# Linear attention ahead of two feed-forward layers: kv by head on 64-column tiles, mean squares on 32-column tiles, k and v loaded by head

## The chip, the cores and the metric

One core of a Trainium2 chip runs the whole program in one launch. The metric is the device time of one execution in microseconds; the time of before is the median of three runs.

## What is computed

For each of 8 batches and 8 heads (576 positions, 64 columns a head) the attention is linear: no softmax, a 64x64 matrix kv of each head, and a root-mean-square norm of each output row. Two feed-forward layers without bias follow.

```python
def _attn_ref(q, k, v, g_norm) -> np.ndarray:
    kv = np.einsum('bhsd,bhse->bhde', k, v)
    out = np.einsum('bhsd,bhde->bhse', q, kv)
    rms = np.sqrt(np.mean(out * out, axis=-1, keepdims=True) + 1e-06)
    return (out / rms * g_norm).astype(np.float32)
...
    x = np.ascontiguousarray(attn_out.transpose(0, 2, 1, 3)).reshape(B * S, H * D)
    x = _moe_ref(x=x, **moe_kwargs)      # (max(0.01*h, h) @ w_out), h = x @ w_in
    return _moe2_ref(x=x, **moe2_kwargs) # ((h - tanh(h)) @ w_out), h = x @ w_in
```

There are 4608 tokens, a model width of 512 and a hidden width of 2048; the four weight matrices come as 64-bit floats and are converted on the chip.

## The kernel before, in words

**The large products.** Each up- and down-projection is cut into blocks of two by two that are multiplied with seven products instead of eight (`PROD`, `NOP = 7`), and every f32 operand is split into two f16 parts, so that one product is a row of f16 matmuls on the whole 128x128 array (`three`, L483 to L493). `up` (L576) runs over superblocks of tokens and 8 pieces of the hidden width, 64 steps of seven products in the first layer; `down` (L641) likewise. Their results leave the banks by ScalarE (`keep`, L518) and VectorE (`add`, L531).

**The attention.** A pair of heads is worked at once (`pair`, L760). Its steps are, on TensorE: `kv` (L765), six f32 matmuls that contract 96 positions each, with both heads' k as the 128 stationary columns and both heads' v as the 128 moving ones, of whose 128x128 result only the two diagonal 64x64 blocks are used; `qtr` (L785), the transposes of q in two halves of 288 positions; `o` (L802), the output of one half with the block-diagonal kv; and `m` (L821), the mean of squares of one half, a matmul with a selecting matrix `sel` that adds the squares of one head into one row of the bank `pm`. A batch has four pairs, and `pm` collects 16 rows (8 heads by two halves) over them. After the last pair `norms` (L843) takes the root on ScalarE, three reciprocals on VectorE, stores the result to DRAM (`store`, L858), reads it back broadcast over 64 partitions in eight loads (`load`, L862), multiplies on GpSimd and splits the result into the f16 operands of the first up-projection.

**What sets the order.** All instructions are recorded in an order that a planner (`Plan`, L44) makes from assumed durations; each engine, and SyncE's DMA queue, works its list in that order and waits by semaphores. The first batch and the second stand ahead of the first product (`early_pair`, L946). The 24 pairs of batches 2 to 7 are woven into the first up-projection: `extra` (L968) puts the seven steps of a pair behind the products n0 + `OFFS` (L969), and `between1` (L987) adds their assumed durations `D_KV`, `D_Q`, `D_O`, `D_M` (L745) to the planner's time of TensorE. Loads of weight words, their conversion and their splitting are spread over that same planned time (`spread`, L1007 to L1013), some of them up to its end.

**The loads.** `load_pair` (L747) puts k, v and q of a pair into tiles of 96 partitions with 6 positions each, the two heads side by side within a position, by one DMA a head:

```python
            held[nm] = L.take([CP, NC, 2, D], F32, nm)
            for h in range(2):
                nc.sync.dma_start(
                    out=held[nm].ap[:, :, h], in_=src[b, 2 * c + h].rearrange("(p c) d -> p c d", p=CP)
                )
```

The matmul of `m` has 16 output rows; the program as built places it on a tile of 128 rows by 32 columns of the array already before the change, all other matmuls of `pair` on the whole array.

Of the kernel before, what the change touches and what calls it, by code (L numbers as in the profile page):

```python
# [11 lines left out]
F32 = mybir.dt.float32  # L12
# [17 lines left out]
P = 128  # L30
# [100 lines left out]
def body(ctx, tc, q, k, v, g_norm, w1, w2, w3, w4, out):  # L131
# [10 lines left out]
    NS2 = NT // (2 * T2)  # L142
    NU = 4 * P
    NL, NM, NX = 20, 11, 13

# [23 lines left out]

    ivd = [scratch([2 * H, T1], F32, f"iv_{b}") for b in range(B)]  # L170
    x1d = {(c, s): scratch([P, 2 * T1], F32, f"x1_{c}_{s}") for c in range(DM // P) for s in range(NS1)}
# [20 lines left out]
    mw = const.tile([P, 4, 2 * NP], F32, name="mw")  # L192
    sel = const.tile([P, 4 * H - 2], F32, name="sel")
    kvd = [const.tile([P, P], F32, name=f"kvd{n}") for n in range(2)]

    def constants():
        for h in range(2):
            nc.sync.dma_start(out=gcol[D * h:D * h + D, :], in_=g_norm.rearrange("(p o) -> p o", o=1))
        make_identity(nc, ident)
        nc.vector.memset(ones, 1.0)  # L200
        nc.vector.memset(eps_sb, EPS / (X_SCALE * X_SCALE))
        nc.vector.memset(sel, 0.0)
        for n in range(2):
            nc.vector.memset(sel[D * n:D * n + D, 2 * H - 2 + n:2 * H - 1 + n], 1.0 / D)
            nc.vector.memset(kvd[n], 0.0)
        nc.vector.tensor_reduce(out=gabs, in_=gcol, axis=AX.X, op=ALU.max, apply_absolute_value=True)
# [537 lines left out]
    PAIRS = (0, 2, 1, 3)  # L744
    D_KV, D_Q, D_O, D_M = 1.6, 0.7, 0.6, 0.55  # L745

    def load_pair(b, c, held):  # L747
        for nm, src in (("k", k), ("v", v), ("q", q)):
            held[nm] = L.take([CP, NC, 2, D], F32, nm)
            for h in range(2):  # L750
                nc.sync.dma_start(
                    out=held[nm].ap[:, :, h], in_=src[b, 2 * c + h].rearrange("(p c) d -> p c d", p=CP)
                )
# [6 lines left out]
    def pair(b, c, held):  # L760
# [4 lines left out]
        def kv():  # L765
            held["pk"], held["bank"] = att_bank("pk")
            for a in range(NC):
                nc.tensor.matmul(
                    out=held["pk"][:, :P], lhsT=two_heads(held["k"], a), rhs=two_heads(held["v"], a),
                    start=(a == 0), stop=(a == NC - 1),  # L770
                )

        def kv_after(e):
            def go():
                held["kvd"] = kvd[kv_n[0] % 2]
                kv_n[0] += 1
                for h in range(2):
                    r = slice(D * h, D * h + D)
                    nc.scalar.activation(out=held["kvd"][r, r], in_=held["pk"][r, r], func=AF.Copy)
                used.discard(held["bank"])  # L780
                L.give(held["k"])
                L.give(held["v"])
            plan.do("A", e + 0.15, 0.5, go)
# [36 lines left out]

        def m(r):  # L821
            first, last = (c == PAIRS[0] and r == 0), (c == PAIRS[-1] and r == 1)
            if first:
                pm[b] = bank(5, "pm")
            row = H * r + 2 * c
            nc.tensor.matmul(
                out=pm[b][:2 * H, :T1], lhsT=sel[:, 2 * H - 2 - row:4 * H - 2 - row], rhs=sq[r].ap,
                start=first, stop=last,
            )
            X.give(sq[r])  # L830

        def m_after(r, e):
            if c == PAIRS[-1] and r == 1:
                norms(b, e)
# [3 lines left out]
            (D_Q, lambda: qtr(1), lambda e: q_after(1, e)), (D_O, lambda: o(0), lambda e: o_after(0, e)),  # L838
            (D_O, lambda: o(1), lambda e: o_after(1, e)), (D_M, lambda: m(0), lambda e: m_after(0, e)),
            (D_M, lambda: m(1), lambda e: m_after(1, e)),  # L840
        ]

    def norms(b, e):  # L843
        held = {}

        def root():
            held["iv"] = X.take([2 * H, T1], F32, "iv")
            nc.scalar.activation(
                out=held["iv"].ap, in_=pm[b][:2 * H, :T1], func=AF.Sqrt,
                bias=eps_sb[:2 * H], scale=1.0 / (X_SCALE * X_SCALE),  # L850
            )
            used.discard(5)
# [9 lines left out]
        def load(kk):  # L862
            held[kk] = L.take([P, 4, T1], F32, "bc")
            rows = ivd[b].rearrange("(r h) t -> h r t", r=2)
            for n in range(2):
                for h in range(2):
                    nc.sync.dma_start(
                        out=held[kk].ap[D * h:D * h + D, 2 * n:2 * n + 2],
                        in_=rows[2 * (kk + 2 * n) + h:2 * (kk + 2 * n) + h + 1].broadcast_to((D, 2, T1)),
                    )  # L870
# [75 lines left out]
    def early_pair(b, c, t, held):  # L946
        gaps = (0.0, 1.7, 2.5, 3.4, 4.4, 5.2, 6.2)
        for (dur, fn, after), g_ in zip(pair(b, c, held), gaps):
            at(t + g_, fn)
            after(t + g_ + dur)  # L950
# [17 lines left out]
    extra = {}  # L968
    OFFS = (1, 4, 6, 8, 10, 12, 14)  # L969
    loads = []  # L970
# [270 lines left out]
```

## Time and profile before

| | |
|---|---|
| median of three runs | 1646.12 us (1645.23 to 1646.91) |
| the profiled execution's own time | 1649.15 us |
| its span, first to last instruction | 1647.4 us |
| TensorE matmuls busy | 1512.3 us, 92% |
| VectorE, ScalarE, GpSimd busy | 1301.6, 867.2, 746.0 us |
| granted TensorE clock, mean | 0.959 |
| DMA packets, of them under 512 B | 251578, 129440 |
| DMA, share of 16 engines | 62.7% |

Busy matmul time counts each matmul from its start to its modelled end, and matmuls overlap, so what the array takes for a group of them is better read from the starts of neighbouring groups. A wait in the profile is the idle time of an engine ahead of an instruction, with what ended it. A queue of SyncE ("SPq") only issues transfers; the time from issue to landing is not in its rows.

### The profile page before, as it was taken

The numbers are of one execution on the slowest core, as the hardware profiler recorded it, in microseconds if no ns is written. First come the engines' busy times: TensorE is split into PE (matmuls) and PEld (weight loads), VectorE is DVE, ScalarE is ACT, GpSimd is POOL, SyncE is SP. The second block draws the span as 40 slices with busy tenths as digits, with TensorE's granted clock in tenths as the row PEclk, the third lists the DMA queues.
The fourth block names the chain that finished last, engine by engine and source line by source line (L and its number), as shares of the span: only waits on it lengthen the run. The fifth ranks groups of instructions, "written<-read, shape, count | busy, mean of one in ns | idle before, by whom it ended". The sixth has DMA issues, their size and how long they took to land. (4 is left out here: it accounts for less than half of the span.)

```text
span 1647.4 us, 32120 instructions
## 1 busy us (share of the span) xinstructions
PE 1512.3 (92%) x12274; PEld 1227.4 (75%) x12274; DVE 1301.6 (79%) x2113; ACT 867.2 (53%) x1381; POOL 746.0 (45%) x758
## 2 busy tenths in 40 slices
PE   5299898898989999999999979999999889999998
PEld 3156675666767777777777768888888778888887
DVE  4765676576667778889989669999999988888881
ACT  3366454465655664444444246666776645455441
POOL 0356203144143345666656134446887654444440
PEclk8589999999999999999999989999999999999999
DMA  9856897898896885545455565555666844444441
GB/s 210 172 88 160 227 239 208 245 245 235 252 259 209 282 318 168 185 145 200 155 172 173 184 233 206 186 210 196 243 240 243 316 143 143 157 129 135 145 132 33
DMA packets 251578, 322.08 MB, mean 196 GB/s; under 512 B 129440, under 2 KB 194080, under 8 KB 251424
## 3 DMA queue, kind: packets, MB, share of 16 engines
q1 hardware_dynamic: 251424, 320.03, 62.7%
q8 instruction: 96, 1.57, 0.4%
q14 instruction: 58, 0.48, 0.1%
HBM read 190.84 MB, written 129.12 MB: 194 GB/s over the span
## 5 line engine op out<-in xcount | busy, mean ns | idle before, releaser
L489 PEld LDWEIGHTS <-w 128*128 128x128 f16 x8400 | 824.8, 99 | 280.1 <-issue 98.7
L468 POOL TENSOR_TENSOR gl<-gl 128x256 f32<-128x256 f32 (+1 forms) x272 | 309.5, 1138 | 307.2 <-issue 79.9
L489 PE MATMUL ps_c<-ops,w 128*128 128x288 f16 (+1 forms) x2400 | 337.3, 285 | 40.2 <-DVE g L536 28.2
L489 PE MATMUL ps_a<-ops,w 128*128 128x288 f16 (+1 forms) x2400 | 333.6, 284 | 22.2 <-ACT u L527 10.3
L489 PEld LDWEIGHTS <-ops 128*128 128x128 f16 x1728 | 169.8, 98 | 28.8 <-issue 7.7
L372 POOL TENSOR_TENSOR unit<-unit 128x128 f32<-128x128 f32 x192 | 134.1, 699 | 116.0 <-DVE wo L365 97.4
L489 PE MATMUL ps_b<-opa,w 128*128 128x288 f16 (+1 forms) x1200 | 170.2, 287 | 0.0
L489 PE MATMUL ps_a<-opa,w 128*128 128x288 f16 (+1 forms) x1200 | 166.8, 283 | 2.9 <-DMA w<-wd 2.8
L489 PE MATMUL ps_d<-opa,w 128*128 128x288 f16 (+1 forms) x1200 | 165.9, 282 | 2.7 <-DVE g L536 2.7
L468 DVE TENSOR_TENSOR gl<-gl 128x256 f32<-128x256 f32 (+1 forms) x272 | 156.0, 576 | 3.3
L874 POOL TENSOR_TENSOR xg<-xg,bc 128x1152 f32<-128x1152 f32 x16 | 43.1, 2694 | 254.3 <-DMA bc<-iv 208.7
L1145 POOL TENSOR_TENSOR g<-g,th 128x512 f32<-128x512 f32 x72 | 101.0, 1403 | 95.9 <-ACT th L1142 95.7
L431 ACT ACTIVATE ops<-gl,inv 128x1024 f16<-128x1024 f32 x72 | 82.6, 1147 | 110.2 <-POOL gl L468 102.9
L489 PEld LDWEIGHTS <-opa 128*128 128x128 f16 x1296 | 126.8, 98 | 16.6 <-issue 1.9
L429 ACT ACTIVATE ops<-gl 128x1152 f16<-128x1152 f32 x64 | 74.3, 1162 | 99.5 <-POOL gl L468 94.6
L438 DVE SCALAR_TENSOR_TENSOR ops<-gl,inv,ops 128x1024 f16<-128x1024 f32 x72 | 104.4, 1451 | 15.8 <-ACT ops L431 15.4
L436 DVE TENSOR_TENSOR ops<-gl,ops 128x1152 f16<-128x1152 f32 x64 | 99.8, 1559 | 19.9 <-ACT ops L429 19.7
L365 DVE SCALAR_TENSOR_TENSOR wo<-unit,s_w,wo 128x384 f16<-128x384 f32 (+1 forms) x96 | 83.4, 871 | 27.1 <-ACT wo L362 26.7
L489 PE MATMUL ps_c<-w,ops 128*128 128x256 f16 x864 | 98.4, 275 | 3.8 <-DVE osb L536 3.8
L489 PE MATMUL ps_a<-w,ops 128*128 128x256 f16 x864 | 96.1, 273 | 3.2 <-ACT u L527 3.2
L468 POOL TENSOR_TENSOR x1g<-x1g 128x256 f32<-128x256 f32 x72 | 68.1, 946 | 65.1 <-DMA x1g<-x 34.7
L438 DVE SCALAR_TENSOR_TENSOR opa<-gl,inv,opa 128x768 f16<-128x768 f32 x72 | 87.2, 1211 | 12.5 <-ACT opa L431 12.5
(118 smaller groups left out, 2192.3 us busy)
## 6 DMA issues: line engine op xcount, KB each, us to landing
g<-g SPq DMA_DIRECT2D x64, 576.0 KB, 4.4
gl<-g SPq DMA_DIRECT2D x64, 576.0 KB, 4.7
g<-g SPq DMA_DIRECT2D x72, 512.0 KB, 3.0
gl<-g SPq DMA_DIRECT2D x72, 512.0 KB, 4.5
wd<-wo SPq DMA_DIRECT2D x48, 448.0 KB, 2.8
w<-wd SPq DMA_DIRECT2D x24, 896.0 KB, 7.4
words<-in_moe_w_in_dram SPq DMA_DIRECT2D x64, 256.0 KB, 5.0
words<-in_moe_w_out_dram SPq DMA_DIRECT2D x64, 256.0 KB, 4.0
```

What stands on the lines that cost most here:

```text
L365: nc.vector.scalar_tensor_tensor(out=dst()[:, 1, a:b], in0=cols(0, n), scalar=scale(), in1=dst()[:, 0, a:b], op0=ALU.mult, op1=ALU.subtract,)
L372: nc.gpsimd.tensor_tensor(out=o, in0=a, in1=b, op=ALU.subtract)
L429: nc.scalar.activation(out=o, in_=i_, func=AF.Copy)
L431: nc.scalar.activation(out=o, in_=i_, func=AF.Identity, scale=scale())
L436: nc.vector.tensor_tensor(out=o, in0=i_, in1=h, op=ALU.subtract)
L438: nc.vector.scalar_tensor_tensor(out=o, in0=i_, scalar=scale(), in1=h, op0=ALU.mult, op1=ALU.subtract)
L468: lambda: e.tensor_tensor(out=g()[:, o], in0=g()[:, a], in1=g()[:, b], op=op),
L489: nc.tensor.matmul(out=out_, lhsT=a, rhs=c, start=start and m == 0, stop=stop and m == n - 1, skip_group_check=not fresh,)
L874: nc.gpsimd.tensor_tensor(out=x, in0=x, in1=held[kk].ap, op=ALU.mult)
L1145: e.tensor_tensor(out=g()[:, n], in0=g()[:, n], in1=held["t"].ap[:, n], op=ALU.subtract)
```

## The change

- `load_pair`: k and v lie in their tiles head by head (96 x 2 x 6 x 64), so that a partition's six positions of one head are one run of 1536 B on both sides of the DMA; q stays as it was.
- `kv`: one matmul of each head with 64 stationary and 64 moving columns in place of one with 128 by 128 for both; head 0 on the array's columns 0 to 63, head 1 on 64 to 127, into partitions 0 to 63 and 64 to 127 of the bank, alternating; 12 f32 matmuls instead of 6.
- `m`: both halves in one step, on array columns 0 to 31 and 32 to 63; `pm`, the inverse norms and their DRAM tile get 64 rows (32 a half, of which 8 are used) instead of 16.
- The planner's durations and slots: kv 0.9 instead of 1.6, a transpose 0.5 instead of 0.7, the one m 0.7 instead of two of 0.55; six steps a pair behind products 1, 4, 6, 8, 10 and 13 instead of seven behind 1, 4, 6, 8, 10, 12 and 14.

```diff
+    Q = 32
...
-    ivd = [scratch([2 * H, T1], F32, f"iv_{b}") for b in range(B)]
+    ivd = [scratch([2 * Q, T1], F32, f"iv_{b}") for b in range(B)]
...
-    sel = const.tile([P, 4 * H - 2], F32, name="sel")
+    sel = const.tile([P, 2 * Q - 2], F32, name="sel")
...
-    D_KV, D_Q, D_O, D_M = 1.6, 0.7, 0.6, 0.55
+    D_KV, D_Q, D_O, D_M = 0.9, 0.5, 0.6, 0.7
...
-            held[nm] = L.take([CP, NC, 2, D], F32, nm)
+            apart = nm != "q"
+            held[nm] = L.take([CP, 2, NC, D] if apart else [CP, NC, 2, D], F32, nm)
...
-                    out=held[nm].ap[:, :, h], in_=src[b, 2 * c + h].rearrange("(p c) d -> p c d", p=CP)
+                    out=held[nm].ap[:, h] if apart else held[nm].ap[:, :, h], in_=src[b, 2 * c + h].rearrange("(p c) d -> p c d", p=CP)
...
             for a in range(NC):
-                nc.tensor.matmul(
-                    out=held["pk"][:, :P], lhsT=two_heads(held["k"], a), rhs=two_heads(held["v"], a),
-                    start=(a == 0), stop=(a == NC - 1),
-                )
+                for h in range(2):
+                    nc.tensor.matmul(
+                        out=held["pk"][D * h:D * h + D, :D], lhsT=held["k"].ap[:, h, a], rhs=held["v"].ap[:, h, a],
+                        start=(a == 0), stop=(a == NC - 1), tile_position=(0, D * h), skip_group_check=True,
+                    )
...
-                    nc.scalar.activation(out=held["kvd"][r, r], in_=held["pk"][r, r], func=AF.Copy)
+                    nc.scalar.activation(out=held["kvd"][r, r], in_=held["pk"][r, :D], func=AF.Copy)
...
-        def m(r):
-            first, last = (c == PAIRS[0] and r == 0), (c == PAIRS[-1] and r == 1)
+        def m():
+            first, last = c == PAIRS[0], c == PAIRS[-1]
...
-            row = H * r + 2 * c
-            nc.tensor.matmul(
-                out=pm[b][:2 * H, :T1], lhsT=sel[:, 2 * H - 2 - row:4 * H - 2 - row], rhs=sq[r].ap,
-                start=first, stop=last,
-            )
-            X.give(sq[r])
+            for r in range(2):
+                nc.tensor.matmul(
+                    out=pm[b][Q * r:Q * r + Q, :T1], lhsT=sel[:, Q - 2 - 2 * c:2 * Q - 2 - 2 * c], rhs=sq[r].ap,
+                    start=first, stop=last, tile_position=(0, Q * r), skip_group_check=True,
+                )
+                X.give(sq[r])
...
-            (D_O, lambda: o(1), lambda e: o_after(1, e)), (D_M, lambda: m(0), lambda e: m_after(0, e)),
-            (D_M, lambda: m(1), lambda e: m_after(1, e)),
+            (D_O, lambda: o(1), lambda e: o_after(1, e)), (D_M, m, m_after),
...
-        gaps = (0.0, 1.7, 2.5, 3.4, 4.4, 5.2, 6.2)
+        gaps = (0.0, 1.2, 2.0, 2.9, 3.9, 5.7)
...
-    OFFS = (1, 4, 6, 8, 10, 12, 14)
+    OFFS = (1, 4, 6, 8, 10, 13)
```

How the instructions move, first on TensorE, at the first products of the up-projection (ps_a and ps_b are the products' banks, pk the bank of kv, pm that of the mean squares; the last pair of the second batch ends here and the first woven one begins). Before:

```order
L489 MATMUL ps_b<-opa,w_0_688 128x288
L768 MATMUL pk<-v,k 128x128 x6
L826 MATMUL pm<-sq,sel 16x288
L489 LDWEIGHTS w_0_688
L489 MATMUL ps_a<-ops,w_0_688 128x288
```

and with the change:

```order
L490 MATMUL ps_b<-opa,w_0_712 128x288
L829 MATMUL pm<-sq,sel 32x288 x2
L771 MATMUL pk<-v,k 64x64 x12
L490 LDWEIGHTS w_0_712
L490 MATMUL ps_a<-ops,w_0_712 128x288
```

Before, the first half's pm stood one product earlier and the second half's stood alone behind kv; now both halves stand together, here ahead of kv.

Second, on SyncE's DMA queue, around the store of the second batch's inverse norms (iv), the broadcast loads that read it (bc), the loads of a pair (k, v, q), of weight words, and the stores of results (g1) and converted weights (wf). Before:

```order
L302 DMA words_1772<-in_moe_w_out_dram 128x2x256 x2
L751 DMA k_1800<-in_k_dram 96x6x64 x2
L751 DMA v_1803<-in_v_dram 96x6x64 x2
L751 DMA q_1806<-in_q_dram 96x6x64 x2
L859 DMA iv_2_71<-iv_1741 16x288
L867 DMA bc_1837<-iv_2_71 64x2x288 x4
L606 DMA g1_0_7_116<-g_1643 128x1152
L347 DMA wf_1_0_1_246<-unit_1763 128x512
L867 DMA bc_1877<-iv_2_71 64x2x288 x4
L302 DMA words_1883<-in_moe_w_out_dram 128x2x256 x2
```

and with the change:

```order
L303 DMA words_1821<-in_moe_w_out_dram 128x2x256 x2
L753 DMA k_1867<-in_k_dram 96x384 x2
L753 DMA v_1870<-in_v_dram 96x384 x2
L753 DMA q_1873<-in_q_dram 96x6x64 x2
L861 DMA iv_2_71<-iv_1796 64x288
L869 DMA bc_1910<-iv_2_71 64x2x288 x4
L303 DMA words_1941<-in_moe_w_out_dram 128x2x256 x2
L869 DMA bc_1948<-iv_2_71 64x2x288 x4
L348 DMA wf_1_0_0_245<-unit_1834 128x512
L607 DMA g1_0_7_116<-g_1710 128x1152
```

The next words now stand between the two groups of broadcast loads instead of behind them, and the stores of results and weights come later. From the end of the first up-projection on, every engine's list is the same as before.

## Rows read from the trace of the kernel before

**Rows 1.** Busy time by stretches; behind the clock: share of 16 DMA engines, GB/s

```profile
core 0: us, PE busy (x) PEld busy (x) DVE busy (x) ACT busy (x) POOL busy (x), PEclk, DMA share, GB/s
0.00:47.00 47.00, 29.31 (x103) 19.93 (x104) 23.23 (x61) 15.53 (x36) 0.70 (x6) 0.78 0.93 219
47.00:58.00 11.00, 0.54 (x2) 0.00 (x0) 11.00 (x29) 5.30 (x8) 0.00 (x0) 0.61 0.49 151
...
80.00:100.00 20.00, 15.28 (x59) 8.84 (x59) 11.74 (x15) 11.76 (x26) 16.59 (x25) 0.65 0.85 115
105.00:590.00 485.00, 449.97 (x3324) 332.79 (x3324) 326.62 (x635) 275.33 (x529) 157.59 (x183) 0.96 0.80 231
```

**Rows 2.** TensorE's waits, 105 to 590 us: total us, times, longest

```profile
PE ps_c L489 <- DVE g L536: 18.5, 8, 5.9
PE ps_a L489 <- ACT u L525: 9.1, 3, 3.8
```

**Rows 3.** ScalarE's waits that a late load or GpSimd ended, same stretch

```profile
ACT wo L362 <- DMA unit<-wf: 22.4, 3, 8.8
ACT opa L429 <- POOL xg L874: 14.3, 10, 3.5
ACT unit L314 <- DMA words<-in_moe_w_out_dram: 13.6, 3, 8.2
```

**Rows 4.** SyncE's DMA queue in order of time: start, us of issuing, count

```profile
169.41 0.33 SPq L606 DMA_DIRECT2D g<-g  x1
...
172.80 1.27 SPq L751 DMA_DIRECT2D k<-in_k_dram  x2
...
177.12 0.83 SPq L859 DMA_DIRECT2D iv<-iv  x1
181.06 2.57 SPq L867 DMA_DIRECT2D bc<-iv  x4
```

**Rows 5.** All engines in order of time, 186 to 197 us; in brackets: idle before

```profile
188.57 1.23 SPq L302 DMA_DIRECT2D words<-in_moe_w_out_dram  x2
...
194.56 0.67 ACT L314 ACTIVATE unit<-words 128x512 f32<-128x512 f32 x1 [8.20 <-DMA words<-in_moe_w_out_dram]
```

**Rows 6.** TensorE in order of time, 300.5 to 318 us: start, us to the modelled end

```profile
300.58 0.91 PE L489 MATMUL ps_a<-ops,w 128*128 128x288 f16 x6
301.42 0.66 PE L826 MATMUL pm<-sq,sel 128*16 128x288 f32 x2
302.01 0.91 PE L489 MATMUL ps_c<-ops,w 128*128 128x288 f16 x6
302.75 0.90 PE L489 MATMUL ps_b<-opa,w 128*128 128x288 f16 x6
...
304.92 1.50 PE L768 MATMUL pk<-v,k 96*128 96x128 f32 x12
306.26 0.90 PE L489 MATMUL ps_d<-opa,w 128*128 128x288 f16 x6
...
311.91 0.65 PE L804 MATMUL po<-qt,kvd 128*128 128x288 f32 x2
312.39 0.90 PE L489 MATMUL ps_d<-opa,w 128*128 128x288 f16 x6
```

**Rows 7.** TensorE's waits, 0 to 67 us

```profile
PE pk L768 <- DMA v<-in_v_dram: 10.8, 2, 7.9
```

**Rows 8.** In order of time: ScalarE's first split of weights, TensorE's first product

```profile
67.38 0.61 ACT L362 ACTIVATE w<-w1f,s1g 128x384 f16<-128x384 f32 x1 [12.58 <-DVE s1g L268]
...
105.32 0.90 PE L489 MATMUL ps_a<-opa,w 128*128 128x288 f16 x6
```

**Rows 9.** Loads of weights: group of products, and by tile (ns min/median/max)

```profile
L489 PEld LDWEIGHTS <-w 128*128 128x128 f16 x8400 | 824.8, 99 | 280.1 <-issue 98.7
...
L768 PEld LDWEIGHTS pk<-v,k x384: 186/192/338, 7.9 to 491.9; 96*128 96x128 f32 x192
...
L826 PEld LDWEIGHTS pm<-sq,sel x128: 92/95/151, 14.0 to 504.0; 128*16 128x16 f32 x128
```

More of the change, by code (lines that the diff above doesn't have):

```diff
@@ L203, in constants @@
         for n in range(2):
-            nc.vector.memset(sel[D * n:D * n + D, 2 * H - 2 + n:2 * H - 1 + n], 1.0 / D)
+            nc.vector.memset(sel[D * n:D * n + D, Q - 2 + n:Q - 1 + n], 1.0 / D)
             nc.vector.memset(kvd[n], 0.0)
@@ L819, in o_after, with m_after @@
             plan.do("V", end, 0.46, copy)
-        def m(r):
-            first, last = (c == PAIRS[0] and r == 0), (c == PAIRS[-1] and r == 1)
+        def m():
+            first, last = c == PAIRS[0], c == PAIRS[-1]
             if first:
                 pm[b] = bank(5, "pm")
-            row = H * r + 2 * c
-            nc.tensor.matmul(
-                out=pm[b][:2 * H, :T1], lhsT=sel[:, 2 * H - 2 - row:4 * H - 2 - row], rhs=sq[r].ap,
-                start=first, stop=last,
-            )
-            X.give(sq[r])
-        def m_after(r, e):
-            if c == PAIRS[-1] and r == 1:
+            for r in range(2):
[4 more added lines that the diff above has]
+                X.give(sq[r])
+        def m_after(e):
+            if c == PAIRS[-1]:
                 norms(b, e)
@@ L846, in root @@
         def root():
-            held["iv"] = X.take([2 * H, T1], F32, "iv")
+            held["iv"] = X.take([2 * Q, T1], F32, "iv")
             nc.scalar.activation(
-                out=held["iv"].ap, in_=pm[b][:2 * H, :T1], func=AF.Sqrt,
-                bias=eps_sb[:2 * H], scale=1.0 / (X_SCALE * X_SCALE),
+                out=held["iv"].ap, in_=pm[b][:2 * Q, :T1], func=AF.Sqrt,
+                bias=eps_sb[:2 * Q], scale=1.0 / (X_SCALE * X_SCALE),
             )
@@ L863, in load @@
             held[kk] = L.take([P, 4, T1], F32, "bc")
-            rows = ivd[b].rearrange("(r h) t -> h r t", r=2)
+            rows = ivd[b].rearrange("(r q) t -> q r t", r=2)
             for n in range(2):
```

## The prediction

> **What bounds the kernel now.** I read the busy time by stretches first [rows 1]. The program has two parts for this change: everything up to 105 us, in which the first batch's attention and the first weights are prepared, and the first up-projection from 105 to 590 us, in which the attention of batches 2 to 7 is woven between the products. Behind 590 us the order of every engine's instructions is the same as before, so what is gained or lost ahead of it is carried to the end. In the 485 us of the up-projection TensorE is busy 450 us: it is the bound. What it idles there shows in its waits [rows 2]: the two largest groups hold 27.6 us, and they name VectorE and ScalarE. Those two are not slow, they are held up: ScalarE idles for loads that come late [rows 3], 22.4 us for halves of weights, 13.6 us for weight words and 14.3 us for the scaled attention output, which itself waits for a load. ScalarE and VectorE work their lists in order, so a late load at the head of the list holds back the evictions behind it, and TensorE waits for a bank. One such place is told in full by the list of the DMA queue [rows 4] and the engines beside it [rows 5]: around 172 to 191 us the queue issues loads of the next pair, the store of the inverse norms, the broadcast loads and then weight words; the words issued at 188.57 us are what ScalarE had been idle for 8.20 us for, up to 194.56 us. So two things cost time here: TensorE's own stream, and the crowded DMA queue.
>
> **TensorE, kv.** The stream is read from a quiet stretch [rows 6]. Six products with 288 columns take 0.74 us (302.01 to 302.75). The twelve matmuls of one kv (six f32 matmuls, two instructions each) take 306.26 - 304.92 = 1.34 us, 0.112 each, with no gap ahead or behind. After the change there are 24 instructions with half the columns, so 0.056 us each. If the two heads' tiles work at once, each head's chain is 12 x 0.056 = 0.67 us, and the second starts one instruction later: 0.73 us. If they don't, it is 24 x 0.056 = 1.34 us. To this comes a change of tile shape on the way in and out. The kernel has one already: the matmul of the mean squares writes 16 rows and is built on a 128x32 tile, and it takes 302.01 - 300.58 - 0.74 = 0.69 us, while two f32 matmuls of the same 288 columns on the whole array (o, 311.91 to 312.39) take 0.48. The difference, 0.21 us, is 0.10 ahead (the six products from 300.58 end their stream at 301.32, pm starts at 301.42) and 0.11 behind. I take it for kv too: 0.73 + 0.21 = 0.94 us, a gain of 0.40; without overlap 1.55, a loss of 0.21.
>
> **TensorE, mean squares.** Now 2 x 0.69 = 1.38 us a pair. After the change both halves stand in one place, so one of the two switches goes. Without overlap: 4 x 0.24 + 0.21 = 1.17 us, a gain of 0.21. With overlap I count that the two instructions of one half stay in order on their tile and the other half's first starts with the second of these: 3 x 0.24 + 0.21 = 0.93, a gain of 0.45. No row shows whether two column tiles work at once, that is the main unknown; between 0.85 gained and nothing (0.21 - 0.21) a pair, I take the overlap, because the row nearest to it, pm on its narrow tile, runs its two instructions back to back at the full column rate once the tile shape is set. 24 pairs stand in the up-projection: **24 x 0.85 = 20.4 us less**, bounds 0 and 24 x 1.35 = 32 (both halves in 0.48 us and kv in 0.67, no switch at kv). Loads of weights cost nothing in these counts, since today a product's load of 99 ns [rows 9] is hidden at a pitch of 0.123 us [rows 6]. The Trainium skill (TensorE: Matmul & The Clock Gate, Part 3: Packing small matmuls, on what overlaps) speaks against that: a load overlaps matmuls in flight only where the row groups differ, and here all are the same. The products of this trace disagree for the whole array; for column tiles no row decides. By the rows the term stays at 20.4 us less, by the rule it would be the slow rival's 89 us more. The other eight pairs run ahead of 105 us, where TensorE waits for loads and ScalarE anyway; I cost them at nothing.
>
> **The loads of k and v.** A load of one head of k moves 96 x 6 x 64 x 4 B = 147 KB. Now its pieces are 256 B, after the change each partition's 1536 B are one run on both sides. Between 80 and 100 us hardly anything but such loads is on the queue: 115 GB/s at a share of 0.85, or 135 GB/s at a full share; between 47 and 58 us the pieces are 1 KB: 151 GB/s at 0.49, or 308 [rows 1]. Shares are rough at the edges of a stretch, but a factor of two is safe. Four such loads a pair, 24 pairs, are 14.2 MB: 105 us of full DMA time become 46, out of 0.80 x 485 = 388. The queue's issues get shorter too: a load whose pieces are strided takes 1.27 us for two, a store with one run a partition 0.33 for one [rows 4].
>
> What that is worth in the up-projection is an estimate. The 27.6 us of waits follow from late loads, but part of their chain stays: store of the norms, then broadcast loads, then GpSimd. I take a quarter off, with a little more for TensorE's clock, which was granted at 0.96 on the mean [rows 1], and give back what a faster TensorE adds by arriving earlier: **6 us less**; bounds 17 less (all late words gone) and 10 more. For the "more" speaks that the planner now counts 3.8 us a pair where it counted 5.3 (36 us over the stage), so the second weights' splitting and the third's conversion, spread up to the planned end, fall on fewer products: VectorE's 327 us [rows 1] then lie in some 458 us, 71% instead of 67%. Also m is now at slot 13 instead of 12 and 14, so the norms of a batch start one product sooner, and the words that came behind the broadcast loads now stand between them. The store of the inverse norms has 64 rows instead of 16 (74 KB, half of one k load); it lies on the chain to the broadcast loads, and I count 0.3 us of the 6 against it each time.
>
> Ahead of 105 us the DMA share is 0.93 up to 47 us [rows 1], and TensorE waits 10.8 us for v [rows 7]; behind it VectorE has the converted words to finish, the scale is ready at 67.38 us and the splits of the first weights follow [rows 8]. The 16 loads of k and v of the first batch are 2.36 MB, 17.5 us at 135 GB/s and 7.7 at 308: at most 9.8 us. VectorE's own work (23.2 us in the first 47, then all of 47 to 58) hides about half: **4.5 us less**, bounds 0 and 9.8.
>
> The sum: 20.4 + 6 + 4.5 = 30.9 us less than the profiled execution's 1649.15 us, or 1618.2; the median of the runs, 1646.12, is 3.03 below it, so **1615 us**. Square, copies and evictions keep their sizes; kvd is copied from other columns of the bank, at the same 64x64.
>
> **The rivals.**
> *The tiles don't overlap*, so the change of shape is paid and nothing bought: TensorE 0, the loads' 10.5 us stay: 1635.6 us. Against it speaks only that the pieces are on different columns of the array. A chance of 0.17.
> *Only the mean squares overlap.* For kv each instruction needs its own weights, and a load for 64 f32 columns has the same 0.056 us of columns as its matmul; if loads go one after another, kv stays at 1.55. Then 24 x (0.45 - 0.21) = 5.8 us from TensorE, 16.3 in all: 1630 us. For it: today's kv is as close to its loads as to its matmuls (192 ns a load against 95 for 16 columns [rows 9], so some 0.1 of each is columns). 0.17.
> *Slower: loads no longer hide.* Today's loads are hidden, as said. If on column tiles a load waits until the matmul ahead has left the array, each of kv's 24 instructions costs 0.056 plus a load between 0.095 and 0.192 us, say 0.14: 24 x 0.196 + 0.21 = 4.9 us, and m 4 x (0.24 + 0.095) + 0.21 = 1.55. That is 3.7 us more a pair, 89 us over 24: some 1725 us. It makes the kernel slower from 0.016 us of uncovered load an instruction on (10.5 us over 24 x 28). Against it: pm's second instruction on its narrow tile starts without such a wait, or its 0.69 us would be 0.78. The rule of the Trainium skill quoted above (TensorE: Matmul & The Clock Gate, Part 3) is this case. 0.07.
> *The waits grow instead*, by 10 us, as VectorE's list gets denser and the loads come in a new order: 1631. 0.06. *The waits mostly go*, 17 us: 1604. 0.06.
>
> **How the numbers follow.** The forecast has 0.47: overlap in both places and some relief, 1603 to 1626 by its own bounds. The range 1600 to 1638 adds the rivals up to 1636 and leaves out the slow one and the far ends of the bounds. Differences under 0.2%, about 3 us, can't be told from no change. Faster 0.89, within it 0.03 (a mixture of growing waits and no overlap), slower 0.08 (loads that don't hide, or waits much worse).
>
> **What would show it.** In the changed profile: from the start of a pk group to the next product 0.94 us and for pm 0.93, with the second tile's matmuls starting while the first's run; 1.55 and 1.17 say no overlap, near 5 says uncovered loads. 128 loads x 480 = 61,440 packets fewer; the DMA share of the up-projection near 0.72; the two largest groups of waits near 20 us instead of 27.6; the first product near 101 us instead of 105.32 [rows 8]; the part from the end of the up-projection to the end unchanged within 3 us. If TensorE's pair costs are right and the time is not, the waits or the part behind 590 us must have grown, and I would be wrong on the relief.

## The result, and the profile after

The changed kernel takes **1606.53 us** (median of four runs, 1600.36 to 1607.68) against 1646.51 us for the kernel before in the same set (1645.23 to 1648.07): a ratio of 0.9749, 95% interval 0.9722 to 0.9776. A second set, the same two kernels again below, gave 0.9744 (0.9717 to 0.9772). The forecast of 1615 us was 8.5 us too high, and the time lies inside the range. The profiled execution of the changed kernel is the fastest of the four (1600.36 us, span 1598.6).

By stretches, cut at the first product and at the end of the first up-projection (columns as in [rows 1]):

```profile
0.00:99.00 99.00, 50.60 (x304) 28.53 (x305) 68.65 (x141) 43.23 (x90) 34.06 (x52) 0.71 0.68 179
99.00:546.00 447.00, 418.82 (x3610) 313.45 (x3608) 318.27 (x631) 271.93 (x525) 158.97 (x177) 0.98 0.78 251
546.00:1598.00 1052.00, 1007.10 (x8749) 858.92 (x8746) 908.78 (x1342) 551.60 (x770) 556.76 (x530) 0.99 0.54 183
```

The up-projection takes 447 us instead of 485, 38 us less, where the medians differ by 40. Subtracting TensorE's busy time splits it: busy 449.97 [rows 1] to 418.82, 31 us less; idle 35.0 to 28.2, 7 us less. The stretches ahead and behind are 6 and 4 us shorter here, but those two differences don't hold, as a second profile of the kernel before will show.

TensorE's stream in the quiet stretch (start, us to the modelled end; beside [rows 6]):

```profile
304.14 0.90 PE L490 MATMUL ps_a<-ops,w 128*128 128x288 f16 x6
304.97 0.92 PE L771 MATMUL pk<-v,k 96*64 96x64 f32 x24
305.82 0.91 PE L490 MATMUL ps_d<-opa,w 128*128 128x288 f16 x6
...
315.39 0.90 PE L490 MATMUL ps_c<-ops,w 128*128 128x288 f16 x6
316.21 0.68 PE L829 MATMUL pm<-sq,sel 128*32 128x288 f32 x4
316.83 0.91 PE L490 MATMUL ps_b<-opa,w 128*128 128x288 f16 x6
```

Six products take 0.74 us, so kv takes 305.82 - 304.14 - 0.74 = 0.94 us, switches of tile shape included (1.34 before), and both halves of the mean squares 316.83 - 315.39 - 0.74 = 0.70 (2 x 0.69 before). In the single records of these groups kv's matmuls start in pairs, the two heads' 6 to 8 ns apart and the pairs every 58 ns (the second pair 106 ns behind the first); in pm the first instructions of both halves start 6 ns apart, and the second ones 7. Both column tiles work at once in both places.

TensorE's waits in the up-projection (total us, times, longest; beside [rows 2]), and ScalarE's (beside [rows 3]):

```profile
PE ps_a L490 <- ACT c L526: 9.3, 5, 7.0
PE ps_c L490 <- DVE g L537: 8.9, 6, 3.0
PE ps_a L490 <- ACT u L526: 3.5, 2, 1.9
PE pm L829 <- ACT sq L813: 3.5, 3, 1.3
```

```profile
ACT opa L430 <- POOL xg L876: 16.0, 7, 3.7
ACT wo L363 <- DMA unit<-wf: 11.0, 4, 5.4
...
ACT unit L315 <- DMA words<-in_moe_w_out_dram: 6.0, 8, 2.0
```

The two groups that held 27.6 us hold 12.4, and another has come up, 9.3 us for c, of which one wait is 7.0. The 3.5 us for the squares are new: m now stands one product sooner than the second half's did, and in the place at 302.79 us it is the second half's square that it waited 1.28 us for. ScalarE waits half as long for halves of weights (wo) and for the words of the down-projection, and no less for the scaled attention output (opa, which needs GpSimd's xg, the output times the inverse norms). One wait is new, 8.7 us, for words of the up-projection; with it, ScalarE's waits for weights are 35 us, against 44 before.

DMA packets (all, and under 512 B):

```profile
DMA packets 190525, 322.57 MB, mean 202 GB/s; under 512 B 55712, under 2 KB 133024, under 8 KB 190368
```

61,053 packets fewer than before, where 61,440 were counted; the other 387 are nearly the 8 x 48 rows by which the stores of the inverse norms have grown, which the count left out. Ahead of the first product (ScalarE's first split of weights; TensorE's first product; beside [rows 8]):

```profile
61.31 0.61 ACT L363 ACTIVATE w<-w1f,s1g 128x384 f16<-128x384 f32 x1 [12.09 <-DVE s1g L269]
```

```profile
98.92 0.90 PE L490 MATMUL ps_a<-opa,w 128*128 128x288 f16 x6
```

Up to 60 us TensorE's waits for v hold 10.5 us, as before [rows 7]; over all of the stretch ahead of that product they are 16.0 us, against 17.8 before.

### The profile page after: what moved, and what is told of

It reads as the page before. It is cut to its first block, busy times and chain, and to the rows that moved or that the text cites. A ratio compares the mean times of both kernels' runs of the same rounds, so it can differ in the third digit from the quotient of the medians.

```text
span 1598.6 us, 32852 instructions
## 1 busy us (share of the span) xinstructions
PE 1476.5 (92%) x12658; PEld 1200.9 (75%) x12658; DVE 1295.7 (81%) x2113; ACT 866.8 (54%) x1381; POOL 749.8 (47%) x758
## 5 line engine op out<-in xcount | busy, mean ns | idle before, releaser
L490 PE MATMUL ps_a<-ops,w 128*128 128x288 f16 (+1 forms) x2400 | 331.1, 283 | 23.3 <-ACT u L528 10.5
```

Source lines behind the costliest of these rows:

```text
L490: nc.tensor.matmul(out=out_, lhsT=a, rhs=c, start=start and m == 0, stop=stop and m == n - 1, skip_group_check=not fresh,)
```

## The experiments

Twelve runs were made: ten other kernels, and the two of this document once more. The kernel before, on the chips of these sets, had medians of 1648.72 (the first four experiments), 1648.24 (the next four) and 1647.93 us (the last four); ratios are to those.

### The parts, one at a time

**Loads alone**: the kernel before with k and v loaded head by head. kv reads 128 adjacent columns of the tiles, two positions of one head, so it leaves out the sums that the attention needs and keeps the matmuls' shapes.

```diff
-            held[nm] = L.take([CP, NC, 2, D], F32, nm)
+            apart = nm != "q"
+            held[nm] = L.take([CP, 2, NC, D] if apart else [CP, NC, 2, D], F32, nm)
...
-                    out=held["pk"][:, :P], lhsT=two_heads(held["k"], a), rhs=two_heads(held["v"], a),
+                    out=held["pk"][:, :P], lhsT=flat(held["k"], a), rhs=flat(held["v"], a),
```

> The kernel before with k and v loaded head by head and nothing else; kv's matmuls keep their shapes and read 128 columns that lie side by side in the new tiles (two positions of one head in place of one position of two heads, so kv holds other sums). Theory A, the gains add up: TensorE's stream is unchanged (kv 1.34 us, pm 0.69 us), the first product comes some 5 us earlier and the waits of the up-projection shrink by about 6 to 10 us: 1630 to 1638 us. Theory B, the loads are the main part and TensorE's time is only swapped against waits: 25 us or more off, 1622 us or less. Theory C, the loads were hidden anyway and the rest came from the planner's new numbers: within 4 us of 1646.

**Old loads**: the changed kernel with the loads of before. It has the tiles, and the planner's new durations and slots with them.

```diff
-                        out=held["pk"][D * h:D * h + D, :D], lhsT=held["k"].ap[:, h, a], rhs=held["v"].ap[:, h, a],
+                        out=held["pk"][D * h:D * h + D, :D], lhsT=held["k"].ap[:, a, h], rhs=held["v"].ap[:, a, h],
```

> The changed kernel with the loads of k and v as before (256 B pieces), the matmuls on column tiles and the planner's new numbers kept. Theory A: kv 0.95 us and m 0.71 us a pair stay, that is 25 us off TensorE's stream; the first product near 105 us and the waits as before: 1617 to 1625 us. Theory B: with the DMA queue as crowded as before, waits eat most of the 25 us: 1632 to 1640 us. Theory C as for A, but with fewer waits than before: 1612 us or less.

**Planner's durations alone**: the kernel before, its instructions and slots unchanged.

```diff
-    D_KV, D_Q, D_O, D_M = 1.6, 0.7, 0.6, 0.55
+    D_KV, D_Q, D_O, D_M = 0.9, 0.5, 0.6, 0.35
```

> The kernel before with the planner's durations of the change (kv 0.9, a transpose 0.5, the two mean squares 0.7 together) and nothing else; slots behind the products stay. Theory A and B: the order moves a little, time within 5 us of 1646. Theory C: the new order of loads and conversions is what shortens the waits: 8 us off or more, 1638 us or less.

**Heads in turn**: the changed kernel, head 0's six matmuls and then head 1's.

```diff
-            for a in range(NC):
-                for h in range(2):
+            for h in range(2):
+                for a in range(NC):
```

> The changed kernel with kv's twelve matmuls in another order: first the six of head 0, then the six of head 1, instead of alternating. If two column tiles work at once only where their matmuls stand next to each other in the list, kv goes from 0.95 to about 1.55 us, 24 x 0.6 = 14 us on TensorE, and the time to about 1618 to 1622 us. If TensorE reorders over a longer stretch or each tile has a list of its own, kv stays near 0.95 us and the time within 4 us of 1606.

Measured: loads alone 1638.92 us, ratio 0.9929 (0.9904 to 0.9954); old loads 1614.68, 0.9789 (0.9760 to 0.9818); durations alone 1640.41, 0.9950 (0.9931 to 0.9970); heads in turn 1613.89, 0.9778 (0.9749 to 0.9806). The loads by themselves gain 10 to 12 us (by medians and by the ratio), the durations by themselves 8. The tiles were run by themselves nowhere: the kernel with old loads owes its 34 us to tiles, durations and slots together, and what the durations are worth in it only the kernels further below tell. The up-projection of the loads alone, of the old loads, and of the durations alone (by stretches, as above):

```profile
99.80:584.00 484.20, 447.48 (x3324) 331.03 (x3323) 327.50 (x635) 274.63 (x529) 156.25 (x183) 0.96 0.74 231
```

```profile
101.90:557.60 455.70, 419.73 (x3611) 313.34 (x3610) 317.77 (x631) 271.99 (x525) 158.52 (x178) 0.98 0.83 247
```

```profile
103.70:583.40 479.70, 445.95 (x3323) 329.33 (x3322) 317.74 (x631) 271.65 (x525) 157.32 (x177) 0.98 0.77 232
```

With the loads alone the DMA share of the stage falls from 0.80 to 0.74, yet the stage stays at 484 us and TensorE's idle time at 484.2 - 447.5 = 36.7: the lighter queue buys no wait there. With the old loads TensorE is as little busy as in the change (419.7), and its idle time is 36.0 instead of 28.2. So the loads do take 8 us of waits away once TensorE is faster and the durations are new, and none in the old setting, by one profile of each. The ratios say the same less sharply: 0.9789 and the change's 0.9749 and 0.9744 have intervals that overlap. With the durations alone the idle time is 479.7 - 445.95 = 33.7 us, hardly less than before; what the stage is shorter there is mostly busy time, at a granted clock of 0.98.

kv with the heads in turn (TensorE in order of time):

```profile
301.57 1.43 PE L771 MATMUL pk<-v,k 96*64 96x64 f32 x24
302.94 0.91 PE L490 MATMUL ps_d<-opa,w 128*128 128x288 f16 x6
```

302.94 - 301.57 is 1.37 us, with the switch ahead 1.46 (the median of the 24 in the stage), against 0.94. So the tiles share the time only where their instructions stand close together; with the order in turn, kv is no faster than on the whole array. In the single records a head's instructions start every 58 ns, and only around the change of heads three pairs start 3 to 6 ns apart, so that the first instructions of head 1 run beside the last of head 0. That is 24 x 0.52 = 12 us, and the stage is 462.6 instead of 447. The median is 7 to 9 us above the changed kernel's, fewer than the 12; the ratio's interval overlaps that of the change at its edge. The same records tell of the weight loads: even one after another on one tile, a matmul and its load take 0.058 us, about the time of the matmul's columns alone (0.056).

### The same two kernels again

> The kernel before once more, for a second profile of it: how far the stretches differ between two profiles of one kernel. If the 5 us that the part behind the up-projection is shorter in the changed kernel's profile are the change's work, this part takes 1057 us again; if it is the spread of single executions, it takes 1050 to 1055 us.

> The changed kernel once more beside the two variants below, on their chip: a ratio of 0.972 to 0.978 to the kernel before; first product near 99 us, up-projection 447 us within 3.

Measured: before, in its profiled execution, 1644.54 us; after 1604.66, ratio 0.9744 (0.9717 to 0.9772). Before and after, by stretches:

```profile
0.00:99.60 99.60, 51.59 (x208) 33.16 (x209) 65.86 (x137) 40.17 (x85) 31.13 (x47) 0.73 0.85 177
99.60:586.60 487.00, 452.59 (x3323) 334.22 (x3322) 328.44 (x635) 275.83 (x529) 157.53 (x183) 0.95 0.79 230
586.60:1642.00 1055.40, 1008.74 (x8747) 859.63 (x8744) 907.08 (x1342) 552.56 (x770) 553.35 (x530) 0.99 0.54 183
```

```profile
0.00:98.40 98.40, 49.92 (x304) 28.67 (x305) 68.68 (x141) 43.32 (x89) 33.80 (x52) 0.65 0.69 180
98.40:547.30 448.90, 421.37 (x3611) 314.41 (x3610) 319.46 (x631) 272.25 (x525) 158.73 (x177) 0.97 0.79 250
547.30:1603.00 1055.70, 1006.86 (x8747) 857.26 (x8745) 905.55 (x1342) 550.77 (x770) 552.84 (x530) 0.99 0.54 182
```

The up-projection repeats within 2 us (485 and 487; 447 and 449), its idle time within 0.7 (35.0 and 34.4; 28.2 and 27.5). The stretch ahead does not: the kernel before has its first product at 105.3 in one profile and at 99.6 in the other. And the part behind is 1055 to 1056 us here in both. So of the 48.8 us between the first two spans, 38 are the change's in the up-projection, and one or two profiles say nothing of the rest. Over all profiles the first product starts at 102.6 us on the mean with the old loads (four, 99.6 to 105.3) and at 99.3 with the new ones (ten, 96.3 to 101.9).

### Whose relief is it: the loads' or the planner's?

**Old durations**: the changed kernel, planned with 5.3 us a pair as before instead of 3.8.

```diff
-    D_KV, D_Q, D_O, D_M = 0.9, 0.5, 0.6, 0.7
+    D_KV, D_Q, D_O, D_M = 1.6, 0.7, 0.6, 1.1
```

> The changed kernel with the planner's durations of before (kv 1.6, a transpose 0.7, mean squares 1.1 for both halves); matmuls, loads and slots as changed. Theory A, tiles and loads do it and the planner's numbers only follow: within 4 us of the changed kernel. Theory C, the shorter assumed durations order the loads and conversions better and so shorten the waits (the kernel before gained 8 us by them alone): 6 to 10 us slower than the changed kernel, with the difference in the waits of the up-projection and not in kv and pm.

Measured: 1621.29 us, 0.9839 (0.9817 to 0.9860), some 16 us above the change. kv and m are unchanged (0.94 and 0.70). The up-projection:

```profile
96.30:561.80 465.50, 424.90 (x3612) 317.50 (x3611) 325.19 (x632) 272.29 (x526) 160.08 (x181) 0.95 0.76 241
```

The new durations are thus worth some 16 us in the changed kernel, twice what they are worth in the kernel before; and what tiles and slots add to the lighter loads without them is, by the ratios 0.9929 and 0.9839, some 15 us. Its idle time is 40.6 us, 12 to 13 more than in the change, more even than before. One of the places, all engines in order of time (in brackets: idle before, and what ended it):

```profile
237.45 0.92 ACT L430 ACTIVATE opa<-xg 128x864 f16<-128x864 f32 x1 [6.23 <-POOL xg L876]
...
239.33 0.39 ACT L526 ACTIVATE u<-ps_a 128x288 f32<-128x288 f32 x1
...
239.77 0.90 PE L490 MATMUL ps_a<-ops,w 128*128 128x288 f16 x6 [2.73 <-ACT u L526]
240.13 2.84 POOL L876 TENSOR_TENSOR xg<-xg,bc 128x1152 f32<-128x1152 f32 x1 [2.71 <-DMA bc<-iv]
...
243.00 0.92 ACT L430 ACTIVATE opa<-xg 128x864 f16<-128x864 f32 x1 [3.28 <-POOL xg L876]
...
243.96 1.79 DVE L437 TENSOR_TENSOR opa<-xg,opa 128x288 f16<-128x288 f32 x2 [0.44 <-ACT opa L430]
...
245.67 0.44 DVE L537 SCALAR_TENSOR_TENSOR g<-ps_c,u 128x288 f32<-128x288 f32 x1
...
246.17 1.60 PE L490 MATMUL ps_c<-ops,w 128*128 128x288 f16 x6 [5.50 <-DVE g L537]
```

Two waits stand here. At 239.77 us TensorE has waited 2.73 us for u, which stands behind opa on ScalarE's list; opa had waited 6.23 us for GpSimd's xg. At 246.17 it has waited 5.50 us for g. The last u written ahead of this g was done at 239.72 us already, but on VectorE's list its part of opa (243.96) stands ahead of g; that waits for ScalarE's opa (243.00), which waited 3.28 us for xg, which waited 2.71 us for the broadcast of the inverse norms. Both evictions are held by the norms' chain at the head of a list, not by a weight load. At 181, 306 and 435 us it is otherwise: ahead of those waits ScalarE had waited 3.28, 5.33 and 8.61 us for late words or halves of weights. In the kernel before, the eight gaps in TensorE's stage where two matmuls start over 2.2 us apart stand in six places, near 127, 190, 258, 325, 391 and 457 us: one for each of the six woven batches. With the old durations there are eight again, in six places from 117 to 430; the change has four, at 183, 240, 351 and 481.

**Old durations, loads earlier**: as the last, with every load of halves and words planned 1 us sooner.

```diff
-        plan.chain(t, [(None, 4.5, load), (None, 0.0, room)] + stages + [(None, 0.0, store)])
+        plan.chain(t, [(None, 5.5, load), (None, 0.0, room)] + stages + [(None, 0.0, store)])
...
-    spread(lambda i, kk, t: convert(1, i, kk, t, 6.0), UNITS, START + 52.0, START + 180.0)
+    spread(lambda i, kk, t: convert(1, i, kk, t, 7.0), UNITS, START + 52.0, START + 180.0)
```

> The changed kernel with the old durations (as in the run e7_old_durations, 1621 us) and 1 us more between the issue of a load of weight words or weight halves and the conversion that uses it (6 to 7 and 4.5 to 5.5 us of planned time). If the old durations cost time because a planned microsecond is then worth less than a real one, so that loads reach the head of ScalarE's list too late, the longer lead gives most of it back: 1606 to 1614 us, with ScalarE's waits for loads shorter. If the old durations just make an unlucky order, it stays at 1618 to 1624 us.

Measured: 1617.12 us, 0.9818 (0.9801 to 0.9835), not told apart from the last. ScalarE's waits for loads fall from 36.6 to 18.6 us, TensorE's idle time goes from 40.6 to 43.3. ScalarE's wait for the norms' chain, and the two largest that are left for loads (issue: the profile names nothing that ended it, and it is counted with them):

```profile
ACT opa L430 <- POOL xg L876: 41.7, 12, 6.9
...
ACT wo L363 <- issue: 8.7, 1, 8.7
...
ACT unit L315 <- DMA words<-in_moe_w_in_dram: 4.6, 3, 2.6
```

Where a load is no longer late, ScalarE stands longer before opa (33.4 us with the old lead, 41.7 now; 14.9 in the second profile of the change). So with half of the late loads gone TensorE waits as long: the norms' chain holds the lists in their place.

Late loads do count, though. In the kernel before, eight waits of TensorE are over 1.9 us long, 27.3 us together; ahead of five of them, 17.5 us, ScalarE had just waited 3 to 9 us for words or halves of weights, as in [rows 5], and ahead of the other three for xg. The longest wait of the changed kernel is of the first kind (the queue and the engines in order of time):

```profile
338.00 0.50 SPq L861 DMA_DIRECT2D iv<-iv  x1
342.90 2.84 SPq L869 DMA_DIRECT2D bc<-iv  x4
...
349.40 1.26 SPq L303 DMA_DIRECT2D words<-in_moe_w_in_dram  x2
...
355.40 0.66 ACT L315 ACTIVATE unit<-words 128x512 f32<-128x512 f32 x1 [8.72 <-issue]
...
358.17 1.60 PE L490 MATMUL ps_a<-ops,w 128*128 128x288 f16 x6 [6.97 <-ACT c L526]
```

The second of the words' loads landed at 355.33 us. They were issued late because the queue works its list in order: ahead of them stand two groups of broadcast loads, and these wait until the store of the inverse norms has landed, so that the queue issues nothing from 338.50 to 342.90. In the up-projection it stands 14.8 us in this way before, 13.2 in the change, and 15.5 with the loads alone. So the norms' chain also makes the weight loads behind it late, and lighter loads of k and v don't change that: with the loads alone ScalarE waits as long for halves of weights as before (22.4):

```profile
ACT wo L362 <- DMA unit<-wf: 22.2, 3, 8.7
```

**Shorter durations**: the changed kernel, 3.4 us a pair.

```diff
-    D_KV, D_Q, D_O, D_M = 0.9, 0.5, 0.6, 0.7
+    D_KV, D_Q, D_O, D_M = 0.9, 0.35, 0.55, 0.7
```

> The changed kernel with still shorter durations: a transpose 0.35, an output 0.55 (3.4 us a pair in place of 3.8; the profile shows 3.1). If the waits follow the ratio of planned to real time, about 4 us faster than the changed kernel: 1598 to 1603 us. If the gain of the durations was a matter of one lucky order, anything between 1600 and 1615 us.

Measured: **1597.79 us**, 0.9699 (0.9681 to 0.9716), the fastest median; idle 443.7 - 419.6 = 24.1 us:

```profile
100.40:544.10 443.70, 419.61 (x3611) 314.01 (x3610) 318.76 (x631) 271.44 (x524) 153.36 (x176) 0.97 0.79 251
```

The pair really takes 3.1 us (kv 0.94, m 0.70, two transposes at 0.25, two o at 0.48). Planned at 5.3, 3.8 and 3.4 us the kernel takes 1621, 1605 and 1598. A planned pair that is too long makes the planner's time run ahead of TensorE, and work that is due some microseconds later is put behind too few products: it reaches the head of its list before its data. That fits the three runs and the place shown in the kernel with old durations, but it isn't shown: a longer lead for the norms' chain alone, which would test it by itself, wasn't tried, and the durations alone, on the kernel before, left the idle time nearly as it was.

### What the tiles leave

**m beside kv**: the mean squares on 64-column tiles, the shape of kv, and directly ahead of the next pair's kv.

```diff
-    Q = 32
+    Q = 64
...
-    OFFS = (1, 4, 6, 8, 10, 13)
+    OFFS = (1, 4, 6, 8, 10, 15)
```

> The changed kernel with the mean squares on 64-column tiles too (64 rows a half, of which 8 are used) and put into the slot of the next pair's kv, directly ahead of it. If the change of tile shape is what costs 0.10 us on each side, the two steps together take 0.94 + 0.71 - 0.20 = 1.45 us where they stand together, 24 x 0.2 = 4.8 us less TensorE, so 2 to 5 us faster than the changed kernel; if the 0.10 us belong to each step whatever stands beside it, the steps keep 1.65 us and the time is the same or, as the norms start two products later, up to 6 us slower through longer waits.

Measured: 1600.04 us, 0.9695 (0.9669 to 0.9721). TensorE in order of time:

```profile
303.75 1.60 PE L490 MATMUL ps_c<-ops,w 128*128 128x288 f16 x6 [2.52 <-DVE g L537]
305.14 1.65 PE L490 MATMUL ps_b<-opa,w 128*128 128x288 f16 x6
306.58 1.17 PE L490 MATMUL ps_a<-ops,w 128*128 128x288 f16 x6
307.67 0.71 PE L829 MATMUL pm<-sq,sel 128*64 128x288 f32 x4
308.21 0.87 PE L771 MATMUL pk<-v,k 96*64 96x64 f32 x24
309.01 0.91 PE L490 MATMUL ps_d<-opa,w 128*128 128x288 f16 x6
```

309.01 - 307.67 = 1.34, with the switch ahead 1.43 us for both, against 0.94 + 0.70: one change of shape, 0.21 us, saved each time, or 5 us over 24. The busy time of the stage falls to 412.2 us by its row, 6.7 below the change; 5.6 of that come back as idle time (33.8), and still the kernel is faster than the change: its five times, 1592.95 to 1601.81 us, all lie below the five of the change beside it, from 1602.59 on. Its stage is only 1 to 3 us shorter, so where the rest of some 5 us lies is open.

**m beside kv, loads earlier**: the same with 1 us more lead for the loads, as above.

> The mean squares beside kv on 64-column tiles (e8_m_beside_kv, 1600 us) with 1 us more lead for the loads of weight words and halves, as a candidate for the fastest. If late loads still hold up the lists there, 2 to 6 us faster: 1594 to 1598 us; if its waits now come from the chain of the norms, the same within 3 us.

**q head by head too**: q is loaded as k and v are; its transposes read 128 adjacent columns, so it leaves out the right order of the output's rows.

```diff
-            held[nm] = L.take([CP, 2, NC, D] if apart else [CP, NC, 2, D], F32, nm)
+            held[nm] = L.take([CP, 2, NC, D], F32, nm)
...
-        return t.ap[:, a].rearrange("p h d -> p (h d)")
+        return t.ap.rearrange("p h c d -> p (h c d)")[:, P * a:P * a + P]
```

> The changed kernel with q loaded head by head as well; the transposes keep their shape and read 128 columns that lie side by side (two positions of one head, so the rows of the outputs are mixed up), 30,720 packets fewer. If the loads of k and v were worth 6 to 12 us by relieving the DMA queue, half as many packets less are worth 3 to 6 us: 1598 to 1602 us. If the queue no longer ends any wait that counts, the same within 3 us as the changed kernel, 1602 to 1608 us.

Measured: 1600.24 us, 0.9718 (0.9699 to 0.9737), for the first: nothing gained by the lead. 1600.52, 0.9717 (0.9696 to 0.9738), for q: some 4 us below the change, with intervals that overlap; its up-projection is the same 447.5 us, so if the gain is real it lies elsewhere. No version beats the shorter durations by more than the intervals; the two gains, of m beside kv and of shorter durations, were not run together.

## Why the prediction was right, and where it was not

**kv** came as worked out: 0.94 us, with both switches. The main unknown, whether two column tiles work at once, is settled by the starts of the pairs and by the heads in turn.

**Mean squares: the term that was mis-sized.** The step "the other half's first starts with the second of these: 3 x 0.24 + 0.21 = 0.93" is wrong. The halves don't queue behind one another; both first instructions start within 6 ns, so it is 2 x 0.24 + 0.21 = 0.69, and 0.70 was measured. TensorE's term is 24 x (0.40 + 0.68) = 26 us, not 20.4. The switch of 0.21 us, read from a single kind of place, held for kv, for both halves of m, and for m beside kv.

**Waits: size and sign right, the size by luck.** "6 us less" became 7 by the idle time. The step "The 27.6 us of waits follow from late loads" holds for some two thirds of the long waits before; the rest stood behind the norms' chain. What failed is the step from there to the relief: lighter loads of k and v by themselves leave ScalarE's waits for halves of weights at 22.2 us and TensorE's idle time at 36.7, and with the old durations, loads that are planned earlier halve ScalarE's waits for them and leave TensorE's, since the norms' chain is behind the same places. The relief needs the new durations (without them 40.6 us idle) and the new loads (without them 36.0) together. I had read the planner's new durations as a cost, since the spread work falls on fewer products; they are worth 16 us by themselves in the changed kernel. So the 6 us came out right with a cause that the prediction had counted against them. The rival "the waits grow" is what the kernel with old durations shows, where idle time rose by some 6 us over before. Part of the rest is likely the clock: TensorE's busy time fell by 31 us where the stream explains 26, with the granted clock up from 0.96 to 0.98; the forecast had put that into the 6.

**The other rivals.** No overlap (1635.6) and overlap only in m (1630) are out by the rows of kv and m. The number of "the waits mostly go" (1604) is near the time, but not its mechanism: 28 us of idle time are left. The slower rival, loads that don't hide, is out. Kv's weight loads in the changed kernel (ns min/median/max):

```profile
L771 PEld LDWEIGHTS pk<-v,k x768: 132/138/232, 5.6 to 444.5; 96*64 96x64 f32 x192
```

24 of them, 138 ns each, are 3.3 us, and all of kv takes 0.94. They run beside the matmuls of both tiles, although all have the same rows. The rule of the Trainium skill that the prediction weighed (TensorE: Matmul & The Clock Gate, Part 3: Packing small matmuls), that loads overlap matmuls in flight only where row groups differ, does not hold for column tiles here; the same part also lets a load go ahead into a background weight buffer, and whether that is what happens no row tells. Another page of the Trainium skill (TensorEngine Tiling (Array Packing), Key Properties) says that different tiles load and multiply in parallel and that a change of mode drains the engine; the trace agrees with the first by the starts of the pairs, and a change of shape costs 0.21 us here, which may be that drain but isn't shown to be.

**Loads.** Packets came out as counted, but for the 387 of the longer stores. The DMA share of the stage is 0.78 and not 0.72: its busy time fell from 0.80 x 485 = 388 to 0.78 x 447 = 349 us, by 39 instead of 59, and in the loads alone by 388 - 358 = 30. The factor of two between pieces of 256 B and whole runs, taken from two stretches with other work in them, was too large. Ahead of the first product "4.5 us less" is near the 3.3 between the means of the profiles, which lie within 6 us for one kernel, so it is not more than likely. As a whole the loads are worth 7 us (change against old loads, with overlapping intervals) to 12 (loads alone) by the ratios. In the old setting they don't gain this in the up-projection; where those 12 us lie is open. The part behind the up-projection is unchanged, as expected.

The sum was short by 8.5 us against the median: 5.5 from m; the rest is likely the clock, and lies within what the stretches outside the up-projection vary by.

## What to carry to other kernels

Two small matmuls on different column tiles run at once if their instructions alternate; rows of a group on one tile don't tell this, the starts of single instructions in a run with two tiles do. Count one change of shape for every stretch on tiles, and so put tile work of one shape side by side. Where a planner sets the order from assumed durations, a faster step changes the order of everything else: rerun the new code with the old durations, and vary them, before crediting a gain to the code. And run a lone part both on the old and on the new kernel: the loads bought no wait on the one and 8 us on the other, by one profile of each. Where a queue works its list in order, look at what a late load stands behind before making other loads lighter.

## What the runs showed of the hardware

A long wait can cost TensorE more than its length. After the 5.50 us in the kernel with old durations:

```profile
246.17:249.00 2.83, 2.83 (x13) 1.97 (x13) 2.76 (x6) 1.86 (x3) 2.83 (x4) 0.50 1.00 303
249.00:252.00 3.00, 3.00 (x13) 1.93 (x12) 2.24 (x5) 1.16 (x3) 2.74 (x3) 0.55 0.99 293
```

The granted clock is 0.50, the lower of its two levels (1.2 of 2.4 GHz), and 13 matmuls take 2.83 us. In m beside kv, two groups of six behind a wait of 2.52 us take 1.39 and 1.44 us instead of 0.74, so that wait cost another 1.35 us. Not every wait does this: after the 2.73 us at 239.77 us in the kernel with old durations the six products show the 0.90 us of the full clock, and after the wait of 1.28 us for the squares in the changed kernel the next products keep their 0.75 us. So with the waits goes some clock: between the two profiles of the change and the same kernel with old durations, 12 to 13 us are idle time and 3.5 to 6.1 busy time of the same instructions.

Weight loads of kv are hidden even where twelve of them, 138 ns each, follow one another on one tile: the matmuls start every 58 ns. And the change of tile shape has about the same price for 32 and for 64 columns, 0.21 to 0.22 us by the groups above, of which some 0.09 us lie ahead of the first instruction.
